# Heads, outputs, norms and projections between two attention layers ordered by a list scheduler, and a last test on one partition

## The chip, the cores and the metric

One core of one Trainium2 chip runs the kernel. The metric is the device time of one execution in microseconds (us), the median over several runs. A profiled execution of the same program gives the trace that the lines below come from; its times count from the start of its span.

## The reference

Four layers on x of 2048 tokens by 512 features, with 32 heads of 16 features each. Layers 1 and 3 are softmax attention with the weights A, layers 2 and 4 linear attention with the weights B and a learned feature map:

```python
x = x + A(layernorm(x)); x = x + B(layernorm(x)); x = x + A(layernorm(x)); x = x + B(layernorm(x))

def A(x):                      # q, k, v = x @ wqkv, by heads
    p = softmax(einsum("bhqd,bhkd->bhqk", q, k) * 16 ** -0.5)
    return einsum("bhqk,bhkd->bhqd", p, v) @ wo

def B(x):                      # q, k, v = x @ wqkv, by heads
    pq, pk = (einsum("bhsd,hdf->bhsf", t, w_phi) for t in (q, k))
    phi_q, phi_k = (concatenate([softmax(p), softmax(-p)]) for p in (pq, pk))
    num = einsum("bhqf,bhfd->bhqd", phi_q, einsum("bhsf,bhsd->bhfd", phi_k, v))
    den = einsum("bhqf,bhf->bhq", phi_q, einsum("bhsf->bhf", phi_k)) + 1e-6
    return (num / den) @ wo
```

## The kernel before

The tokens are cut into 16 tiles of 128, and these into four blocks j of 512 (NJ = 4). Most matrix products are done in three passes of f16 high and low parts (PASSES); TensorE (PE) writes to PSUM, which is divided into two bank pairs of a ring "S" (`psS`), one pair "W" (`double`) and two single banks "M" (`psum1`). `banks` deals out the three pairs in turn.

**The attention layers** (`LayerA`). Eight groups of heads; scores on PE (line 1197), exponentials on ScalarE (ACT, line 1204), products with the values on PE (line 1247). A planner at build time (`Plan`) sets their order and weaves in the projections of later groups ("octets"), the norms of finished groups and the output projection, by costs and due times written in the code. `norms_task` finds a bound on the scores of an octet with a reduction over the partitions on POOL, and writes the bound's negative into `okt` (line 952). At the end of the attention each token block is fed to the next layer.

**The linear layers** (`LayerB`). `feed` takes a token tile at a time: it projects keys, values and queries (line 1549), makes the two softmaxes of the feature map (`expo`, `share`, line 1608 and on), and gathers key times value (`kvp`, in the bank pair W). For the last tile, `blocks` copies kvp into block-diagonal weights `kvb`, and `expo` and `share` are run for its queries; `todo` holds the last two query tiles, which must still be turned over (`turn`). `rest` then runs the heads of block 0, the two turns, and the heads of block 1.

**From one layer to the next** (`finish`). For each token block:
- `heads(j)`: 16 products of turned queries with kvb for each of two halves k, into two bank pairs (line 1693); each pair goes through `norm2` (line 644 and on: ACT copies it, VectorE (DVE) transposes 32 by 32, divides by the denominator and transposes back, ACT makes the high part, POOL (GpSimd) the low part of `obB`).
- `o_block`: the output projection for two halves of two tiles each (lines 675 and 686), with a load of the residual xt (line 662), the sum on DVE (line 691) and a store (line 692). xt has three buffers.
- For a following attention layer: `Norm.half` (layer norm: statistics on DVE, the reciprocal root by three Newton steps of small POOL instructions, lines 492 to 526), the scaled rows on ACT (line 567), their transposes on PE (line 580), high part on ACT and low part on DVE (lines 590 and 593).
- `LayerA.feed`: for each block j the projections of keys and queries of the first octet (`head`, line 828; evacuated by `head_evac`, lines 1099 to 1103), the values (`values0`, line 1005), squares on ACT, their row sums by head (`head_norms`, line 1048) and the bound (`head_bound`). `load_head` and `load_rows` copy the rows of keys and queries from `stg` to the tiles `kq` that the scores read (lines 1176 to 1178), `load_shift` the rows of the bound (line 1184). The first maximum needs the keys of all four blocks and the queries of the first three.

Before, PE's order in this stretch is written out (`manual_schedule(engines={E.PE})`), with the pieces of the next blocks handed to `feed`:

```python
            with tc.manual_schedule(engines={E.PE}):
                outp(0)
                heads(2)
                nxt.feed(lns, [
                    (lambda: outp(1, 0), lambda: outp(1), no),
                    (lambda: heads(3), lambda: outp(2), no),
                    (lambda: outp(3, 0), lambda: outp(3), no),
                    (no, no, no)])
```

The other engines, and all engines behind the last layer, have the order that the builder's own scheduler gives. DMA queues (SP's above all) are ordered by that scheduler in both kernels.

**The last test.** `okt` holds a number per attention layer and octet. If one is below `shmin`, a general version of the whole stack runs in a conditional block; here none is, and the block is jumped over. The lowest value is found on 32 partitions, compared, reduced over the partitions on POOL (`anybad`, line 1850) and converted (line 1852) for the engines to load.

Of the kernel before, what the change touches and what calls it, by code (L numbers as in the profile page):

```python
# [20 lines left out]
H = 32  # L21
# [32 lines left out]
EXP = 0.904  # L54
THERE = 0.54
BACK = 1.11
POWERS = 26
LEAD = 8
RING = 4
# [13 lines left out]
def mha_hedgehog_stack(ctx, tc, x_in, a_wqkv, a_wo, b_wqkv, b_wphi, b_wo, out, shmin=SHMIN):  # L73
# [15 lines left out]
    def big(shape, dt, name):  # L89
        return bigp.tile(shape, dt, tag="big", name=name)  # L90
# [384 lines left out]


    class Norm:
        def __init__(self, xts, name):
            self.xts = xts
            self.xnT = big([P, 2, NC4, 512], F16, f"xnT{name}")  # L480
            self.xn, self.par, self.landed = {}, {}, 0

        def stats(self, t0, n, soon=False):
            run(self.stats_parts(t0, n, soon))
# [127 lines left out]
        def all(self):  # L612
            self.turn01()
            self.turn23()
            return self.xnT
# [115 lines left out]
    class Plan:  # L731
# [59 lines left out]

    class Task:
        pass

    class LayerA:
        def __init__(self, li, x_src, x_dst):
# [311 lines left out]
        def head_values(self, j):  # L1108
            self.values0(j, psum1("pv_"))

        def feed(self, lns, work):

            for j, (a, b, c) in enumerate(work):
                ln = lns[j]
                self.xnT.append(ln.xnT)
                ln.turn01()
                a()
                ln.turn23()
                b()
                c()  # L1120
                if j == 2:
                    self.head_norms(0)
                self.head(j, (1, 0) if j < NJ - 1 else (1,))
                if j == 1:
                    self.next_w = self.octet_w(1)
                    self.load_head()
                if j == 2:
                    self.load_rows(0, slice(1024, AHEAD), None, (nc.sync, nc.gpsimd))
                if j > 0:
                    self.head_values(j - 1)  # L1130
            self.feed_end()

        def load_head(self):

            self.alloc_pairs(0)
            self.shs = [self.shift_tile("yb") for _ in range(2)]
            self.oct[0]["sh"] = self.shift_tile()
            self.kq_end = [np_.tile([P, 2, S - AHEAD], F16, tag="yn", name="kqe", bufs=5) for _ in range(2)]
            self.load_rows(0, slice(0, 1024))
            self.load_shift(0, slice(0, AHEAD), None, (0,))  # L1140

# [236 lines left out]
        def attention(self, extra, nxt):  # L1378
# [127 lines left out]
            print("attention", self.li, "powers", len(power), round(pe, 1), "exponentials", len(estart), "late", round(lost, 1), "ready", self.ready)  # L1506
            self.fill.append(self.last_tail(NJ - 1, self.last))
            state["att"], state["whole"] = False, True
            with tc.manual_schedule(engines=COMPUTE):
# [6 lines left out]
            nxt.rest()  # L1516


    class LayerB:
        def __init__(self, x_src, x_dst, name):  # L1520
            self.x_src, self.x_dst, self.name = x_src, x_dst, name

        def begin(self):
            self.wqk = stgp.tile([P, 2, 2, NC4, 512], F16, tag="stg", name="wbqk")
# [10 lines left out]
        def feed(self, j, xnT, between=lambda t: None):  # L1535

            if self.kvp is None:
                self.kvp = double()
                state["whole"] = False
            qT = [big([P, 4, 512], F32, f"qT{j}_{i}") for i in range(2)]  # L1540
            self.qT.append(qT)
            for t in range(4):
                tt = 4 * j + t

                def project(dst, w, passes=(0, 1, 2)):
                    for i in passes:
# [12 lines left out]
                if last:  # L1559
                    f_k = self.expo(pk)  # L1560
                    self.kvb = np_.tile([P, 8, 32], F32, tag="yn", name="kvb", bufs=5)
                    nc.gpsimd.memset(self.kvb, 0.0)
                else:
                    pq = bank("pq")
                    project(pq, lambda b, c: self.wqk[:, 0, b, c, :])
                if self.lateq is not None and tt < NT - 2:
                    self.turn(*self.lateq)
                pv_ = bank("pbv")
                project(pv_, lambda b, c: self.wv[b][:, c, :])
                if self.latek is not None:  # L1570
                    self.gather(*self.latek)
                if last:
                    pq = bank("pq")
                    project(pq, lambda b, c: self.wqk[:, 0, b, c, :], (0, 1))
                pvh = pv_.rearrange("p (h d) -> p h d", d=DH)
                low = lambda: nc.vector.scalar_tensor_tensor(  # L1576
                    vt[:, 1, :, 0:16], pvh, 2.0 ** -8, vt[:, 0, :, 0:16], op0=ALU.mult, op1=ALU.subtract)
                if not last:
                    f_k = self.expo(pk)
                    f_q = self.expo(pq)  # L1580
                nc.scalar.activation(vt[:, 0, :, 0:16], pvh, AF.Copy, scale=2.0 ** -8)
                if last:
# [4 lines left out]
                    self.blocks()  # L1587
                    self.todo = [self.lateq, (tt, self.expo(pq), qT)]
# [12 lines left out]
                between(tt)  # L1601
# [104 lines left out]
        def finish(self, nxt):  # L1706
# [20 lines left out]
            if not isinstance(nxt, LayerA):  # L1727
# [4 lines left out]
                    if j + 2 < NJ:  # L1732
                        heads(j + 2)
                return
            no = lambda: None
            with tc.manual_schedule(engines={E.PE}):
                outp(0)
                heads(2)
                nxt.feed(lns, [
                    (lambda: outp(1, 0), lambda: outp(1), no),  # L1740
                    (lambda: heads(3), lambda: outp(2), no),
                    (lambda: outp(3, 0), lambda: outp(3), no),
                    (no, no, no)])


    og = tc.dram_tile([D, S], F32, name="og")
# [102 lines left out]
    anybad = sp.tile([32, 1], F32, name="anybad", bufs=1)  # L1849
    nc.gpsimd.partition_all_reduce(anybad, bad, 32, bass_isa.ReduceOp.max)  # L1850
    flag = sp.tile([32, 1], I32, name="flag", bufs=1)
    nc.vector.tensor_copy(flag, anybad)
# [40 lines left out]
```

## Time and profile before

| | us |
|---|---|
| median of 3 runs (lowest, highest) | 2511.46 (2510.26, 2515.81) |
| profiled execution | 2509.21 |
| its span | 2507.3 |
| first attention, scores (line 1204) | from about 70 to 1008 |
| last query projection of the first linear layer to the first score of the second attention | 1187.3 to 1322.9 |
| second attention | 1323 to 2256 |
| last query projection of the second linear layer to the last sum | 2430.4 to 2501.0 |

In lines of the profile, L12 is a line of the kernel, `out<-in` are the program's names for tiles, x is a count, and an arrow with a time says what ended an engine's idle time. PEld is the load of weights into PE, which overlaps its matmuls. In a list of waits the three numbers are the total, the count, and the longest, in us. In the chain of work that ended last each line has start, duration and what ran.

### The profile page before, as it was taken

Reading aid. Unit: us, or ns where it says so; the run is one execution under the profiler, and the core shown is the slowest. Engines: PE = TensorE matmul, PEld = TensorE weight load, DVE = VectorE, ACT = ScalarE, POOL = GpSimd, SP = SyncE. Lnnn points to the kernel's source line nnn. Section 1 sums busy time; section 2 is a strip of 40 time slices with the busy share of each in tenths; the row PEclk is TensorE's granted clock in tenths of the full one; section 3 lists DMA queues with packets and bytes.
Section 4 is the critical chain, followed back from the end, with each engine's and each line's share of the span. In section 5 each row is a group of like instructions: output and inputs, shape, how many; then the busy total and the mean of one; then the engine's idle time right before and its main releaser. Section 6 shows DMA issues by size and latency. Waiting matters only on the chain.

```text
span 2507.3 us, 103429 instructions
## 1 busy us (share of the span) xinstructions
PE 2305.4 (92%) x46698; PEld 1086.9 (43%) x46698; DVE 1596.5 (64%) x2867; ACT 2134.8 (85%) x2379; POOL 531.2 (21%) x645
## 2 busy tenths in 40 slices
PE   6999999999999999889889999999998999998998
PEld 4444444444434444444344444444443344444543
DVE  8233457756668355989863666667565762469897
ACT  6899999999999999454438999999999999993553
POOL 3111111121110000456431112111111100005552
PEclk9999999999999999999899999999999999999999
DMA  5312240231045331100133003203300441210003
GB/s 195 67 27 45 48 80 20 43 55 42 3 114 135 115 109 53 51 9 31 63 96 57 16 7 60 36 3 51 65 3 11 83 125 54 70 68 28 10 18 111
DMA packets 114924, 142.85 MB, mean 57 GB/s; under 512 B 64184, under 2 KB 69928, under 8 KB 112168
## 3 DMA queue, kind: packets, MB, share of 16 engines
q1 hardware_dynamic: 113288, 133.38, 21.6%
q8 instruction: 367, 6.01, 1.0%
q0 software_dynamic: 1184, 2.77, 0.3%
q14 instruction: 85, 0.70, 0.1%
HBM read 62.16 MB, written 41.94 MB: 42 GB/s over the span
## 4 chain that ended last, share of the span: by engine, by line
ACT 58%; PE 14%; issue 13%; DVE 12%; POOL 2%; DMA 0%; POOLq 0%; ACTq 0%; DVEq 0%
ACT p L1204 56%; PE double L1247 2%; PE s L1197 2%; DVE su L1619 2%; PE pbv L1549 1%; PE po L686 1%; PE pk L1549 1%; PE pq L1549 1%; DVE f L1611 1%; PE pm L703 1%; POOL f L1628 1%; DVE f L1612 1%; DVE mx L1608 1%; DVE st L492 1%; DVE su L1620 1%
## 5 line engine op out<-in xcount | busy, mean ns | idle before, releaser
L1204 ACT ACTIVATE p<-s 128x1024 f32<-128x1024 f32 x2001 | 1852.0, 1064 | 21.7 <-PE s L1197 19.1
L1197 PE MATMUL s<-kq 49*32 49x512 f16 x15136 | 789.3, 381 | 99.1 <-ACT p L1204 86.1
L1197 PEld LDWEIGHTS <-kq 49*32 49x32 f16 x15872 | 386.0, 89 | 880.6 <-issue 798.5
L1247 PE MATMUL double<-p,v 64*32 64x512 f32 x9064 | 612.8, 591 | 0.0
L1247 PE MATMUL pm<-p,v 64*32 64x512 f32 x6944 | 476.6, 590 | 0.0
L894 POOL TENSOR_TENSOR yt<-yt,yt 128x512 f32<-128x512 f32 x64 | 84.7, 1324 | 762.8 <-DVE yt L891 727.9
L1247 PEld LDWEIGHTS double<-p,v 64*32 64x32 f32 x9064 | 174.0, 106 | 30.9 <-issue 6.4
L1549 PEld LDWEIGHTS <-xnTa 128*128 128x128 f16 x1152 | 110.6, 98 | 154.9 <-DVE f L1612 26.2
L1281 DVE SCALAR_TENSOR_TENSOR xt<-pm,c_oA,xt 128x512 f32<-128x512 f32 x102 | 76.2, 747 | 155.0 <-PE pm L703 151.1
L1014 POOL TENSOR_TENSOR sq<-stg 128x512 bf16<-128x512 f16 x48 | 57.7, 1202 | 476.4 <-DVE stg L922 247.6
L1628 POOL TENSOR_TENSOR f<-f,su 128x1024 f32<-128x1024 f32 x62 | 119.9, 1934 | 128.3 <-DVE su L1622 102.9
L1247 PEld LDWEIGHTS pm<-p,v 64*32 64x32 f32 x6944 | 135.2, 106 | 22.2 <-issue 3.3
L891 DVE STREAM_TRANSPOSE yt<-double 128x512 f32<-128x512 f32 x72 | 47.3, 695 | 110.7 <-PE double L1247 110.6
L1613 ACT ACTIVATE f<-f,c_pB 128x1024 f32<-128x1024 f32 x64 | 72.7, 1148 | 52.6 <-DVE f L1612 45.4
L1549 PE MATMUL pbv<-wbv,xnTa 128*128 128x512 f16 x384 | 91.6, 390 | 21.4 <-DVE f L1612 21.4
L1634 ACT ACTIVATE fk<-f 128x1024 f16<-128x1024 f32 x30 | 31.7, 1057 | 75.4 <-POOL f L1628 75.4
L703 PEld LDWEIGHTS <-wA 64*32 64x32 f16 x4608 | 76.1, 93 | 43.4 <-issue 7.9
L891 DVE STREAM_TRANSPOSE yt<-pm 128x512 f32<-128x512 f32 x56 | 36.8, 696 | 89.9 <-PE pm L1247 89.6
L1549 PE MATMUL pq<-wbqk,xnTa 128*128 128x512 f16 x384 | 88.4, 379 | 1.6 <-DVE vt L1576 1.6
L917 DVE TENSOR_SCALAR tq<-double,c_qk 128x512 f32<-128x512 f32 x28 | 21.0, 749 | 107.0 <-PE double L703 103.7
L1549 PE MATMUL pk<-wbqk,xnTa 128*128 128x512 f16 x384 | 88.1, 379 | 0.0
L1619 DVE TENSOR_REDUCE su<-f 128x64 f32<-128x1024 f32 x64 | 77.5, 1211 | 9.3 <-ACT f L1613 8.6
(319 smaller groups left out, 3084.7 us busy)
## 6 DMA issues: line engine op xcount, KB each, us to landing
kq<-stg SPq DMA_DIRECT2D x168, 128.0 KB
xd<-xt SPq DMA_DIRECT2D x40, 512.0 KB
xt<-xd SPq DMA_DIRECT2D x40, 512.0 KB
v<-vyt SPq DMA_DIRECT2D x384, 16.0 KB
oD<-osp SPq DMA_DIRECT2D x24, 256.0 KB
ob<-oD SPq DMA_DIRECT2D x8, 768.0 KB
xt<-in_A_x_dram SPq DMA_DIRECT2D x8, 512.0 KB
wbqk<-dBqk SPq DMA_DIRECT2D x2, 2048.0 KB
```

The costliest lines, as they stand in the source:

```text
L703: nc.tensor.matmul(ps[h][c, :], w[r, c], x[r], start=(n == 0), stop=(n == of - 1), skip_group_check=True)
L891: nc.vector.transpose(ys[u].rearrange("p a b -> p (a b)"), ps[u])
L894: nc.gpsimd.tensor_tensor(ys[0], ys[0], ys[1], ALU.add)
L1014: nc.gpsimd.tensor_tensor(sq, hi, hi, ALU.mult)
L1197: nc.tensor.matmul(banks2[u][32 * c:32 * c + 32, :], self.side(g, half, 64 * u, 0, kt * P + 32 * c, 32), self.side(g, half, 64 * u, 1, j * ...
L1204: nc.scalar.activation(pt, s, AF.Exp, scale=EXPS)
L1247: nc.tensor.matmul(acc[h][32 * hh:32 * hh + 32, :], self.oct[o]["v"][r, x:x + 32], pt[r, hh % 2, :], start=(kt == 0), stop=(kt == NT - 1), ...
L1281: nc.vector.scalar_tensor_tensor(xt[:, u, :], ps[h], con["oA"], xt[:, u, :], op0=ALU.mult, op1=ALU.add)
L1549: nc.tensor.matmul(dst, xnT[:, a, c, t * P:(t + 1) * P], w(b, c), start=(i == 0 and c == 0), stop=(i == 2 and c == NC4 - 1))
L1613: nc.scalar.activation(f, f, AF.Exp, scale=con["pB"])
L1619: nc.vector.tensor_reduce(su, f[:, r, :], AX.X, ALU.add)
L1628: nc.gpsimd.tensor_tensor(f3, f3, self.part_sums(f3, slice(0, 64), factor), ALU.mult)
```

## The change

`LayerB.flow` takes the place of `rest` and `finish` on the main path (`b1.flow(a2)`, `b2.flow(None)`); the general version keeps them. It describes the work as tasks, generators that yield the engine and cost of their next instruction ("T" for PE, "V" for DVE, "A" for ACT, "P" for POOL), or a condition: `got` waits for a free buffer or bank, `known` for a result. `Flow.run` keeps a clock for each engine and picks, at each step, the engine whose next instruction can start first, and on it, of the tasks that are due within HOLD, the one of lowest rank. The instruction is emitted at that moment, under a manual schedule of all four engines. Ranks are numbers for each kind of work and block (RANKS between the layers, TAIL behind the last). DMA issues are emitted where their task stands and have no cost there.

- `heads` is cut into calls of eight products (k, p), each into one bank pair.
- `out_block` is cut into the four columns c of heads, and runs each column when that part of obB is ready.
- `norm_in` does the layer norm, the transposes and both parts for two tiles.
- `project`, `square`, `values`, `bounds` and `rows` are the pieces of `LayerA.feed`; `rows` loads the first 1024 columns of kq once the keys and queries of blocks 0 and 1 are out, the next 512 after block 2.
- The queries of the last tile are no longer put through `expo` and `share` in `LayerB.feed`, but in `flow` (`query`), as are the two turns.
- `Norm` can get its tile later (`room`); `load_head` can leave out two kinds of tile (`bound_tiles`, `end_tiles`).
- The last test reads partition 0 of okt alone, without the reduction on POOL.

```diff
+HOLD = 0.1
+RANKS = dict(query=(2,) * 4, heads=(12.4, 3.3, 24, 30.4), out=(10.2, 17.5, 30.6, 25.2), ln=(2.3, -16.8, 14.2, 5.8),
+             keys=(29.8, 57, 32.4, 34.4), project=(59.7, 22.9, -4.7, 53.4), values=(56.3, 0.5, 50, 57.4))
+TAIL = dict(query=(5,) * 4, heads=(4.6, 26.6, 16.2, 25.9), out=(11.1, 5.6, 11.5, 25.9))
...
+        def run(self):
...
+                    due = [t for t in mine if t.ready <= c + HOLD]
+                    t = min(due, key=lambda t: (t.rank, t.ready, t.seq)) if due else min(mine, key=lambda t: (t.ready, t.rank, t.seq))
+                    at = max(c, t.ready)
+                    if best is None or at < best[0]:
+                        best = at, t
+                at, t = best
+                self.end = self.clock[t.need[0]] = at + t.need[1]
...
+            F = Flow(S=[0.5, FAR], W=[1.2], M=[0.0] * 2, p=[0.0] * 5, yn=[0.0] * 4, yb=[0.0] * 2, xt=[0.0] * 3, xn=[0.0] * 4,
+                     sq=[0.0] * 4, big=[0.0, 0.0])
...
+            def heads(j, k, p):
...
+                yield F.got(1, "S", "W")
+                kind, ps = pair()
+                yield "T", 0.9
+                for g in range(4):
+                    for i in (2 * p, 2 * p + 1):
...
+            def out_block(j, t2):
+                yield known(ready, (j, 0))
...
+                yield F.got(1, "xt")
+                F.take("xt")
...
+                nc.sync.dma_start(xt, self.x_src[r:r + 2 * P, :].rearrange("(t p) d -> p t d", p=P))
+                yield F.got(1, "S", "W")
+                kind, ps2 = pair()
+                for c in range(NC4):
+                    yield known(ready, (j, c))
+                    yield "T", 1.3
...
+                yield "V", 1.2
+                nc.vector.scalar_tensor_tensor(xt, ps2, con["oB"], xt, op0=ALU.mult, op1=ALU.add)
...
+            def project(j, ten):
+                yield known(halves, (j, 0), (j, 1))
+                yield F.got(1, "S", "W")
...
+            def bounds():
+                keys = [(j, ten) for j in range(NJ) for ten in (1, 0)]
...
+                for i, need in enumerate((keys[0:4], keys[4:7], keys[7:8])):
+                    yield known(sqs, *need)
...
+            def rows():
+                yield known(evac, *[(j, ten) for j in (0, 1) for ten in (1, 0)])
+                nxt.next_w = nxt.octet_w(1)
+                yield F.got(2, "big")
+                F.take("big"), F.take("big")
+                nxt.load_head(False)
+                yield known(evac, (2, 1), (2, 0))
+                nxt.load_rows(0, slice(1024, AHEAD), None, (nc.sync, nc.gpsimd))
...
-    b1.finish(a2)
+    b1.flow(a2)
     a2.attention(None, b2)
-    b2.finish(None)
...
-    lowest = sp.tile([32, 1], F32, name="lowest", bufs=1)
-    nc.vector.tensor_reduce(lowest, okt, AX.X, ALU.min)
-    bad = sp.tile([32, 1], F32, name="bad", bufs=1)
-    nc.vector.tensor_scalar(bad, lowest, shmin, None, op0=ALU.is_lt)
-    anybad = sp.tile([32, 1], F32, name="anybad", bufs=1)
-    nc.gpsimd.partition_all_reduce(anybad, bad, 32, bass_isa.ReduceOp.max)
-    flag = sp.tile([32, 1], I32, name="flag", bufs=1)
-    nc.vector.tensor_copy(flag, anybad)
+    lowest = sp.tile([1, 1], F32, name="lowest", bufs=1)
+    nc.vector.tensor_reduce(lowest, okt[0:1], AX.X, ALU.min)
+    flag = sp.tile([1, 1], I32, name="flag", bufs=1)
+    nc.vector.tensor_scalar(flag, lowest, shmin, None, op0=ALU.is_lt)
     rv = nc.values_load(flag[0:1, 0:1], min_val=0, max_val=1)
```

More of the change, by code (lines that the diff above doesn't have):

```diff
@@ L793, in mha_hedgehog_stack, with __init__, add, pull @@
         pass
+    class Flow:
+        def __init__(self, **free):
+            self.clock = {"T": 0.0, "V": 0.5, "A": 0.5, "P": 0.0}
+            self.free, self.tasks, self.count, self.end = free, [], 0, 0.0
+        def add(self, gen, rank, ready=0.0):
+            t = Task()
+            t.gen, t.rank, t.ready, t.need, t.cond, t.last, t.seq = gen, rank, ready, None, None, None, self.count
+            self.count += 1
+            self.tasks.append(t)
+            self.pull(t)
+        def pull(self, t):
+            while True:
+                try:
+                    need = next(t.gen)
+                except StopIteration:
+                    self.tasks.remove(t)
+                    return
+                if need[0] == "until":
+                    at = need[1]()
+                    if at is None:
+                        t.cond, t.need = need[1], None
+                        return
+                    t.ready = max(t.ready, at)
+                    continue
+                if t.last is not None and t.last != need[0]:
+                    t.ready += 0.25 if t.last == "T" else 0.08
+                t.need = need
+                return
+        def got(self, n, *names):
+            def at():
+                times = sorted(x for name in names for x in self.free[name])
+                return times[n - 1] if len(times) >= n else None
+            return "until", at
+        def take(self, *names):
+            name = min((name for name in names if self.free[name]), key=lambda name: min(self.free[name]))
+            self.free[name].remove(min(self.free[name]))
+            return name
+        def give(self, name, n=1, wait=0.1):
+            self.free[name] += [self.end + wait] * n
+        def run(self):
+            while self.tasks:
+                for t in sorted(self.tasks, key=lambda t: (t.rank, t.seq)):
+                    if t.cond is not None:
+                        at = t.cond()
+                        if at is not None:
+                            t.cond, t.ready = None, max(t.ready, at)
+                            self.pull(t)
+                best = None
+                for e, c in self.clock.items():
+                    mine = [t for t in self.tasks if t.need is not None and t.need[0] == e]
+                    if not mine:
+                        continue
+                    due = [t for t in mine if t.ready <= c + HOLD]
[5 more added lines that the diff above has]
+                self.end = self.clock[t.need[0]] = at + t.need[1]
+                t.ready, t.last = self.end, t.need[0]
+                t.need = None
+                self.pull(t)
@@ L1109, in head_values, with bound_tiles, end_tiles, load_head @@
             self.values0(j, psum1("pv_"))
[L1111 to L1133, printed above, removed]
+        def bound_tiles(self):
+            self.shs = [self.shift_tile("yb") for _ in range(2)]
+        def end_tiles(self):
+            self.kq_end = [np_.tile([P, 2, S - AHEAD], F16, tag="yn", name="kqe", bufs=5) for _ in range(2)]
+        def load_head(self, every=True):
             self.alloc_pairs(0)
-            self.shs = [self.shift_tile("yb") for _ in range(2)]
+            if every:
+                self.bound_tiles()
             self.oct[0]["sh"] = self.shift_tile()
-            self.kq_end = [np_.tile([P, 2, S - AHEAD], F16, tag="yn", name="kqe", bufs=5) for _ in range(2)]
+            if every:
+                self.end_tiles()
             self.load_rows(0, slice(0, 1024))
@@ L1505, in attention @@
             assert not plan.tasks and not events
-            print("attention", self.li, "powers", len(power), round(pe, 1), "exponentials", len(estart), "late", round(lost, 1), "ready", self.ready)
             self.fill.append(self.last_tail(NJ - 1, self.last))
             state["att"], state["whole"] = False, True
+            nxt.fixed = True
             with tc.manual_schedule(engines=COMPUTE):
@@ L1515, in attention @@
                     nxt.feed(j, self.out[j], lambda t: self.pumps(3 if t < 4 else t > 4))
-            nxt.rest()
     class LayerB:
@@ L1521, in __init__ @@
             self.x_src, self.x_dst, self.name = x_src, x_dst, name
+            self.fixed = False
         def begin(self):
```

302 lines of the change are left out of this document (290 added, 12 removed).

## The prediction

> **What bounds the kernel now.** I read the page first (busy shares, chain), then the busy time of the three stretches that the diff touches, then who waits for whom in each.
>
> ```profile
> span 2507.3 us, 103429 instructions
> PE 2305.4 (92%) x46698; PEld 1086.9 (43%) x46698; DVE 1596.5 (64%) x2867; ACT 2134.8 (85%) x2379; POOL 531.2 (21%) x645
> ACT  6899999999999999454438999999999999993553
> ACT 58%; PE 14%; issue 13%; DVE 12%; POOL 2%; DMA 0%; POOLq 0%; ACTq 0%; DVEq 0%
> L1204 ACT ACTIVATE p<-s 128x1024 f32<-128x1024 f32 x2001 | 1852.0, 1064 | 21.7 <-PE s L1197 19.1
> ```
>
> ACT carries the two softmax attentions (the runs of 9 in its row; line 1204 alone is 1852 us). The diff leaves their work as it is, apart from what the last test did in the middle of the second. The rest of the diff lies in the two stretches where ACT's digits fall to 3 to 5: behind the first linear-attention layer (I call it the bridge: from its last query projection to the first scores of the second attention) and behind the second (the tail).
>
> ```profile
> core 0: us, PE busy (x) PEld busy (x) DVE busy (x) ACT busy (x) POOL busy (x), PEclk, DMA share, GB/s
> 1187.30:1322.90 135.60, 112.47 (x825) 54.97 (x825) 102.88 (x193) 55.42 (x77) 53.46 (x145) 0.89 0.27 84
> 2430.40:2501.00 70.60, 61.00 (x464) 23.95 (x464) 60.54 (x97) 29.27 (x41) 23.12 (x18) 0.95 0.31 106
> 2501.00:2507.30 6.30, 0.00 (x0) 0.00 (x0) 0.00 (x0) 0.00 (x0) 0.00 (x0) 0.67 0.26 91
> ```
>
> Columns: length, then busy us of PE, PEld, DVE, ACT, POOL, then the granted clock. In the bridge DVE works 102.88 of 135.60 us (76%) and PE 112.47 at a granted clock of 0.89, which is about 100 us at full clock. In the tail both are at 86%. No engine is full, so both stretches lose time to order. The last 6.30 us are the final store, which the change doesn't touch.
>
> **The bridge.** Its instructions stay nearly the same in kind and number: heads, norms, output projections, layer norms, transposes, projections. What changes is who orders them. Now PE's order is written by hand and the other engines' order is chosen by the builder; afterwards one list scheduler fixes PE, DVE, ACT and POOL together, by a rank for each kind of work and token block. DVE's 102.88 us therefore stay. What can go is DVE's idle time, 32.7 us:
>
> ```profile
> DVE xnTb L593 <- ACT xnTb L590: 9.7, 2, 5.9
> DVE tq L1099 <- PE pqk L828: 7.0, 3, 3.3
> DVE xt L691 <- PE double L686: 6.0, 1, 6.0
> DVE yt L646 <- ACT raw L644: 3.9, 2, 2.9
> DVE xt L691 <- PE po L686: 3.8, 1, 3.8
> ```
>
> The first, third and fifth are waits in the middle of the bridge (together 19.5 us), where other blocks have DVE work that could stand there: the 32 transposes, multiplies and evacuations of four blocks don't depend on each other. The second stands at the end:
>
> ```profile
> 1307.84 1.22 DVE L593 TENSOR_TENSOR xnTb<-double,xnTb 128x1024 f16<-128x1024 f32 x1
> 1307.63 4.44 PE pqk L828 x12
> 1312.07 2.68 PE pv__26758 L1005 x48
> 1314.75 2.60 PE pqk L828 x12
> 1318.13 0.68 DVE nm L1049
> 1320.83 2.06 DMA kq<-sh
> 1322.93 0.55 PE s L1197 x8
> ```
>
> From the end of the last evacuation of normed rows (1309.06) to the first score (1322.93) are 13.9 us. PE puts the values of block 2 (2.68) and the last query projection (2.60) ahead of the row sums whose maximum (line 1049) gives the softmax bound; the new order gives the last key projection a better rank (34.4) than values (50) and that query projection (53.4), so these 5.3 us leave the chain. The key projection takes 4.44 where the same twelve matmuls take 2.60 at full clock: 1.8 more can go. Against it, square and row sums of that last key block now follow one another, some 2 us: the row sums and their maximum take 1.5 now, from the end of the query projection (1317.35) to 1318.81, and half a microsecond is my estimate for the square. So the end would be 13.9 - 5.3 - 1.8 + 2 = 8.8 us.
>
> Floor of the bridge: 102.9 of DVE and nearly all of that end, 8.5 us, 111.4 in all, a gain of 24. The other bound is no gain, or a loss, if the fixed order stalls somewhere. The nearest row for what a simple order reaches is the tail, 60.54 of 70.60: at that share 102.88 need 119.7, a gain of 15.9; half the way to the floor is 12.1. I take 13 (122.6 us), nearer the lower, because PE is as full as DVE: 100 us at full clock plus the same end.
>
> PE's own cost changes at one place. The heads come in calls of eight matmuls on two row groups instead of sixteen on four:
>
> ```profile
> 1187.30:1322.90 135.60, 20.73 (x256) 3.34 (x256) 0.89 0.27 84
> 2433.26 1.09 PE L1693 MATMUL pn<-qT,kvb 32*32 32x512 f32 x16 [0.46 <-DVE f L1612]
> 2460.41 1.14 PE L1693 MATMUL pn<-qT,kvb 32*32 32x512 f32 x32
> ```
>
> A call of eight (16 records) takes 1.09, a call of sixteen 1.14, so all sixteen calls of a layer take 17.4 us split and 9.1 whole. The bridge now has 20.73 us of them, since the halves go apart there already when only one bank pair is free. I cost the split at nothing; if PE were the only bound and the whole calls could be had, it would be 8.3.
>
> The clock is a second place. In two stretches of the bridge:
>
> ```profile
> 1220.00:1230.00 10.00, 5.42 (x39) 1.95 (x40) 5.87 (x12) 5.69 (x7) 4.97 (x27) 0.50 0.33 106
> 1260.00:1270.00 10.00, 10.00 (x49) 5.12 (x49) 10.00 (x18) 4.47 (x6) 3.00 (x3) 0.96 0.00 0
> ```
>
> Where PE is half idle the granted clock is 0.50, where it is full 0.96. I let the 0.89 of the whole stand in the sum: with it PE has 112 us and is the tighter of the two bounds. [...]
>
> **Queues.** SP's order isn't fixed by the scheduler, but its work is moved:
>
> ```profile
> 1279.78 1.30 SPq L1176 DMA_DIRECT2D kq<-stg  x1
> 1287.57 0.59 SPq L1178 DMA_DIRECT2D kq<-stg  x1
> 1224.74 0.37 SPq L662 DMA_DIRECT2D xt<-xd  x1
> ```
>
> The first rows of keys and queries are twelve copies on SP, from 1279.78 to 1288.16, 8.4 us. They need the queries of block 0, whose rank (59.7) is the worst of all. Now they lie 35 us ahead of the first score and cost nothing. If that evacuation came last, the first score would follow it by 8.4 and the 2.06 of a landing, 10.5 us, against 8.8 for the chain of the bound: 2 us more, within what I left of the floor. On POOL the six later copies stand in the fixed order behind the evacuations of block 2; what waits behind them is the layer norm's small arithmetic of block 3, but POOL has 53.46 busy of 135.60 us, so I cost them at nothing, and at their own issue time, some 3 us, if a norm stands right behind them. The eight loads of xt (0.37 to issue) have no time in the scheduler's model. Six matmuls for each of four columns stand before their first use; they are the rival that makes the kernel slower.
>
> **The tail.** The same work without layer norms.
>
> ```profile
> DVE xt L691 <- PE po L686: 7.9, 2, 4.0
> 2491.26 8.39 PE po L686 x38
> 2499.67 1.28 DVE xt L691
> ```
>
> DVE has 60.54 of 70.60 us; 7.9 of its idle time are the last two output blocks, for which PE still has 38 matmuls (8.39 us) when the last head is ready. The new order runs the columns of both output blocks as they come, so that only the last column of each is left, two times 1.3 (a block half has 24 matmuls, 8.39 / 38 x 24 = 5.3 us, and a column is a quarter of it). Floor: 60.5, 1.7 at the start, and 4.4 at the end: 66.6, a gain of 4. PE has 61.00 at a clock of 0.95, 58 us, and can't start its outputs before the first heads are normed, so the floor is hardly reached. No gain is the other bound, 2 lost if a column waits in the fixed order. I take 2.
>
> **The last test.** Now a partition reduction on POOL and a conversion behind it; afterwards a minimum on one partition and a comparison that writes the integer. The builder puts the old one not at the end but into the second attention, at 1927 to 1942:
>
> ```profile
> POOL yt L894 <- issue: 7.2, 1, 7.2
> DVE flag L1852 <- POOL anybad L1850: 7.2, 1, 7.2
> POOL anybad L1850 <- issue: 6.0, 1, 6.0
> ACT p L1204 <- PE s L1197: 6.0, 2, 4.9
> PE double L1197 <- DVE yt L891: 4.9, 1, 4.9
> ```
>
> Read from below: PE waits 4.9 us for a transpose on DVE, which stands behind the flag, which waits 7.2 us for the reduction, ahead of which POOL has 6.0 us without a record; ACT, the bound there, stands 6.0 us. POOL needs another 7.2 us before its next add. In the whole of each attention ACT waits for scores this long:
>
> ```profile
> ACT p L1204 <- PE s L1197: 6.5, 14, 1.2
> ACT p L1204 <- PE s L1197: 12.5, 9, 4.9
> ```
>
> The first is the attention without that test, the second the one with it; they differ by the same 6.0. Without reduction the flag follows the minimum at once, the transpose runs when its bank is full, and the 6.0 go; the minimum still waits for the last bound on POOL, which costs DVE 4 us that nothing needs. The bounds are 0 (the builder puts the new instructions where they stall something else) and 7.3 (a later wait of 1.3 goes as well). I take 6.0. The two new instructions cost two short ones on DVE in place of three.
>
> **The sum.** 13 + 2 + 6 = 21 us off the profiled execution, 2509.2 us with 1.9 around its span: 2488.2. The median of the three runs shown is 2511.5, 2.3 above it, so I predict 2490.5, rounded 2490. A measurement of this kernel can tell about 0.2%, 5 us, from no change.
>
> **Rivals.**
> - The bridge comes to its floor because PE keeps its full clock: 24 + 4 + 6 = 34, 2477. For it: the rows of the clock, and independent work in plenty. Against: three bank pairs have to carry heads, outputs, transposes and projections, and no stretch of this kind here exceeds 86%. Chance 0.10.
> - The fixed order stalls head-on as often as the present one: one late instruction holds its whole engine. The bridge gives 3, the tail nothing, the test 6: 2502. For it: PE's order has been fixed already and lost 23 us in the bridge. Chance 0.20.
> - Slower: loads of xt. With three buffers the loads of five of eight output halves can only start when an earlier half is through its norm. A half megabyte at the 84 to 106 GB/s of these stretches is 5 to 6.2 us, and DVE, in its fixed order, stands still for what isn't covered. It eats the gain of 21 from 4.2 us uncovered for each of the five, and is slower by 0.2% from 5.2; uncovered in full at 5.4 it gives 27, 2517. Against: each load is issued before 5.3 us of matmuls of its own block. Chance 0.05.
> - The change doesn't do what it says: the new minimum still holds DVE where PE needs it, and the bridge stays where it is: 2511 within 0.2%. For it: the wait of the minimum for POOL stays. Chance 0.09.
>
> **How the numbers follow.** My forecast has 0.56. Faster by over 0.2% are it and the first two rivals, 0.86, of which I give 0.01 to the slower side for a stall that I haven't named: 0.85, 0.09, 0.06. The forecast's own range, by a bridge gain of 7 to 19 and a tail of 0 to 4, is 2482 to 2498. The range from 2477 to 2504 takes in both faster rivals and leaves out the last two.
>
> **What would show it.** Bridge: under 125 us from the last query projection to the first score, DVE's share over 80%, PE's clock over 0.93, and no values between the last key projection and its row sums. Tail: the wait of xt for po under 4 us. Test: no anybad, and ACT's wait for scores in the second attention 6 to 7 us. Wrong would be a DVE wait for a load of xt, a first score that waits for rows of stg instead of the bound, or a bank wait that holds PE while DVE is idle.

## The result and the profile after

The changed kernel took 2495.93 us (median of 6 runs, 2493.94 to 2498.00), the kernel before 2512.52 (6 runs beside them): 16.6 us less, ratio 0.9934 [0.9921, 0.9947]. On a second chip it was 2495.67 against 2516.21, ratio 0.9925 [0.9906, 0.9944] (e12_after_2 below; a ratio is worked out from all runs of both kernels and can differ from the quotient of the medians). The forecast was 21 off the profiled execution, 2490, in a range of 2477 to 2504.

Stages of profiled executions, cut as in the prediction, but with the bridge up to the first exponential (0.5 us behind the first score). "Feed" is a linear layer up to its last query projection. Attention and feeds of other executions of the same code are beside them to show how well such a row repeats:

| us | before | after | again on another chip |
|---|---|---|---|
| to the end of the first attention | 1008.77 | 1009.35 | 1010.08 |
| feed of the first linear layer | 178.56 | 178.33 | 178.48 |
| bridge | 136.17 | 124.02 | 124.94 |
| second attention | 933.22 | 928.12 | 929.53 |
| feed of the second linear layer | 173.68 | 175.33 | 175.08 |
| tail | 70.55 | 70.64 | 69.47 |
| final store | 6.35 | 6.41 | 6.42 |
| span | 2507.3 | 2492.2 | 2494.0 |

The bridge gave 12.15 and the second attention 5.1; the tail gave nothing here, and 1.65 went in a feed whose code the change hardly touches. Two of these rows move by themselves: over all profiled executions here the second feed took 173.6 to 175.7, and the second attention 933.2 to 937.7 with the old test (five executions) and 926.2 to 931.0 with the new one (nine).

The page of the changed kernel, and the busy time by stage (length, then PE, PEld, DVE, ACT, POOL, then the granted clock):

```profile
span 2492.2 us, 103433 instructions
PE 2303.5 (92%) x46698; PEld 1083.9 (43%) x46698; DVE 1602.2 (64%) x2866; ACT 2136.6 (86%) x2379; POOL 530.6 (21%) x644
ACT  6899999999999999444539999999999999993553
```

```profile
1187.70:1311.20 123.50, 106.24 (x825) 51.81 (x825) 107.18 (x191) 55.65 (x77) 54.12 (x145) 0.94 0.22 67
2415.50:2485.80 70.30, 63.29 (x464) 23.83 (x448) 62.41 (x96) 29.54 (x41) 22.57 (x18) 0.95 0.26 91
2485.80:2492.20 6.40, 0.00 (x0) 0.00 (x0) 0.00 (x0) 0.00 (x0) 0.00 (x0) 0.77 0.25 90
```

In ACT's row the last slice between the attentions goes from 8 to 9 tenths; a slice is 62 us, so 12 us shows as no more. Engines do the same work. In the bridge DVE's share went from 76% to 87%, PE's clock from 0.89 to 0.94, and its busy time fell by 6.2 us with the same 825 matmuls. DVE's own busy time rose by 4.3 us, so its idle time fell from 32.7 to 16.3. What DVE still waits for in the bridge:

```profile
DVE xnTb L603 <- ACT xnTb L600: 5.1, 2, 3.2
DVE xt L1953 <- PE fl L1950: 3.4, 2, 3.1
DVE nm L1132 <- PE psn L1131: 2.2, 1, 2.2
DVE tq L2047 <- PE double L911: 1.0, 1, 1.0
```

The waits of 9.7, 7.0, 6.0, 3.9 and 3.8 us of before are 5.1 and 3.4 (xnTb, xt), 1.6 (tq, 0.6 of it in a further line for `fl`), and none (yt). No wait for a load of xt is among them. The end of the bridge, from the chain of work that ended last:

```profile
1296.66 1.03 ACT xnTb L600
...
1297.74 2.75 PE double L911 x12
1300.49 2.59 PE fl L911 x12
1303.08 2.68 PE pv__26779 L1088 x48
1305.76 0.77 PE psn L1131 x3
...
1306.55 0.68 DVE nm L1132
...
1308.97 2.12 DMA kq<-sh
...
1311.13 0.55 PE s L1266 x8
```

PE goes through the key projection (`double`, 2.75), the query projection (`fl`, 2.59), the values (2.68; they are those of block 3 now) and only then the row sums. The last evacuation of normed rows ends at 1298.95, the first score starts at 1311.13: 12.2 us, against 13.9 before.

The tail, the end of its chain and DVE's waits:

```profile
2476.79 0.49 POOLq L2241
2477.28 0.71 POOL obB L1930
...
2478.04 1.25 PE fl L1950 x5
2479.29 5.19 PE double L1950 x24
...
2484.51 1.28 DVE xt L1953
```

```profile
DVE xt L1953 <- PE double L1950: 3.9, 1, 3.9
DVE xt L1953 <- PE fl L1950: 2.9, 3, 1.3
```

The last output half has all its 24 matmuls (5.19) behind the other one's last column; DVE waits 3.9 us for them. In all it waits 6.8 for outputs here, 8.1 before; the prediction wanted under 4.

The last test, and ACT's wait for scores from the end of the bridge on, with the longest one (4.8) that for the first score itself:

```profile
1917.85 0.15 DVE L2238 TENSOR_REDUCE lowest<-okt 1x1 f32<-1x8 f32 x1 [4.09 <-POOL okt L1035]
1918.04 0.14 DVE L2240 TENSOR_SCALAR flag<-lowest 1x1 int32<-1x1 f32 x1
```

```profile
ACT p L1273 <- PE s L1266: 7.4, 7, 4.8
```

The minimum still holds DVE for 4.09 us, and nothing but DVE pays for it: beside it ACT runs 18 exponentials without a gap (1909.15 to 1925.91). The first score has no such wait of 4.8 in the kernel before (2.0); without it ACT waits 2.6 here and waited 10.5 before.

### The profile page after: what moved, and what is told of

The parts are those of the page before. It is cut to its first block, busy times and chain, and to the rows that moved or that the text cites. A ratio compares the mean times of both kernels' runs of the same rounds, so it can differ in the third digit from the quotient of the medians.

```text
span 2492.2 us, 103433 instructions
## 1 busy us (share of the span) xinstructions
PE 2303.5 (92%) x46698; PEld 1083.9 (43%) x46698; DVE 1602.2 (64%) x2866; ACT 2136.6 (86%) x2379; POOL 530.6 (21%) x644
## 4 chain that ended last, share of the span: by engine, by line
ACT 58%; PE 14%; issue 12%; DVE 12%; POOL 2%; DMA 0%; ACTq 0%; POOLq 0%; SPq 0%; DVEq 0%
ACT p L1273 57%; PE double L1316 3%; PE s L1266 2%; DVE su L1691 1%; PE pbv L1618 1%; PE pk L1618 1%; PE pq L1618 1%; PE pm L713 1%; DVE yt L1908 1%; DVE f L1683 1%; POOL f L1700 1%; DVE f L1684 1%; PE fl L1950 1%; DVE mx L1680 1%; PE pm L1316 1%
## 5 line engine op out<-in xcount | busy, mean ns | idle before, releaser
L1700 POOL TENSOR_TENSOR f<-f,su 128x1024 f32<-128x1024 f32 x58 | 112.2, 1934 | 116.3 <-DVE su L1694 103.4
L1950 PE MATMUL fl<-wbo,obB 128*128 128x512 f16 x312 | 76.7, 403 | 8.7 <-ACT raw L1902 3.6
```

What stands on the lines that cost most here:

```text
L1700: nc.gpsimd.tensor_tensor(f3, f3, self.part_sums(f3, slice(0, 64), factor), ALU.mult)
L1950: nc.tensor.matmul(ps2[:, u, :], obs[j][:, c, a, t * P:(t + 1) * P], wo[:, b, c, :], start=(c == 0 and i == 0), stop=(c == NC4 - 1 and i = ...
```

## The experiments

The ratios are to the kernel before, run on the same chip. Theory throughout: three independent gains, bridge about 12, test about 5, tail none.

### e1_test: the last test alone

```diff
-    lowest = sp.tile([32, 1], F32, name="lowest", bufs=1)
...
-    nc.gpsimd.partition_all_reduce(anybad, bad, 32, bass_isa.ReduceOp.max)
...
+    lowest = sp.tile([1, 1], F32, name="lowest", bufs=1)
+    nc.vector.tensor_reduce(lowest, okt[0:1], AX.X, ALU.min)
```

> The kernel before with the last test on one partition and nothing else. Theory: the POOL reduction in the second attention held DVE and through it PE; without it ACT's idle time there falls, and the second attention gets shorter by the 5.2 us that it lost in the changed kernel (933.3 to 928.1 from first to last exponential): 5 us off the time. Rival: the gain came from somewhere else in the new bridge (another start of the second attention), and the test alone gives under 2 us.

2507.51 (9 runs) against 2513.66 (25 runs), ratio 0.9975 [0.9965, 0.9985]: 6.2 us. The second attention took 926.48 (933.22 before). ACT's wait for scores in it:

```profile
ACT p L1204 <- PE s L1197: 6.2, 6, 2.6
```

12.5 became 6.2. The prediction's 6.0 stands.

### e2_bridge: the scheduled bridge alone

```diff
-    b2.flow(None)
+    b2.finish(None)
```

and the old test.

> The list scheduler between the first linear layer and the second attention alone; old tail, old test. Theory: the bridge is 123.5 us instead of 135.6, all else as before: 12 us off. Rival: a part of the 12 us is given back when the second attention starts (rows of keys that come late), so that the time falls by 8 or less.

2513.79 (11 runs), ratio 1.0003 [0.9994, 1.0012]: nothing, though the bridge was 124.96. The tail, whose code is that of before, took 80.19 in place of 70.55, and the second attention 937.65, the longest of the five with the old test. What PE and ACT wait for in this tail:

```profile
PE double L1767 <- ACT raw L654: 11.5, 3, 5.6
```

```profile
ACT raw L654 <- PE pn L1767: 11.0, 2, 9.7
```

And in the chain:

```profile
2466.98 10.47 PE po L696 x48
2478.74 1.03 ACT raw L654
```

Of block 3 the halves of heads had only begun when 48 output matmuls of earlier blocks got ahead of them: ACT, which copies the heads, stood 9.7 us. Both theories missed this, and the parts aren't independent. `banks` deals out the three bank pairs by a counter; the old bridge draws 40 pairs from it, the scheduled one none (it names its pairs itself). In the attention and in the linear layer's feed the counter is switched off (`whole`), so the old tail goes on from where the bridge left it. 40 is 1 more than a multiple of 3, so that tail gets its pairs in another turn. The next two runs test that.

### e5_bridge_turn and e6_before_turn: the counter alone

```diff
+    state["turn"] = (state["turn"] + 1) % 3
```

behind the scheduled bridge (e5), and by 2 ahead of the second attention in the kernel before (e6).

> The scheduled bridge alone, as in the run before it, with one step added to the counter that deals out the three bank pairs in turn. The old bridge drew 40 pairs from that counter, the scheduled one draws none, so that the old tail began one step off (40 is 1 more than 3 times 13) and took 80.2 us instead of 70.6. Theory: with the step put back the tail is 70.6 us again and the time falls by 9 to 10 us against the bridge alone, to about 2504. Rival: the tail was longer for another reason (its order by the builder hangs on times further back), it stays near 80 us and the time near 2513.

> The kernel before, with the counter of bank pairs set two steps on ahead of the second attention and nothing else changed. Theory: its tail starts at the place in the turn that the run with the scheduled bridge alone had, takes 80 us instead of 70.6, and the kernel gets 9 to 10 us slower (2523). Rival: no change.

e5: 2502.72 (8 runs) against 2515.29 (13 runs), ratio 0.9957 [0.9942, 0.9972], tail 70.64. e6: 2524.78 (5 runs), ratio 1.0041 [1.0029, 1.0054], tail 80.15, with the same wait to the tenth:

```profile
ACT raw L644 <- PE pn L1693: 11.0, 2, 9.7
```

So one turn of a round robin is worth 9.6 us in the old tail, and the bridge by itself, with the counter put right, is worth 12.6 by the medians and 10.8 by the ratio. The scheduled tail chooses its own pairs: in the full change it doesn't gain over the old one, but it keeps away the 9.6 that the scheduled bridge would have brought upon it.

### e3_tail: the scheduled tail alone

> The list scheduler behind the last linear layer alone; old bridge, old test. Theory from the trace of the changed kernel: the tail stays at 70.6 us, no change within 1 us. Rival, the step of the prediction: 2 us off.

2511.67 (11 runs), ratio 0.9995 [0.9985, 1.0004]; tail 69.62. No gain that can be told from none by the times. The stage shows a little: five executions with the scheduled tail as in the changed kernel took 69.5 to 70.6 (69.8 on average), three with the old one in its usual turn 70.6 to 70.8.

### e4_xt: the last output half

```diff
-                    F.give("xt", 1, 4.0)
+                    F.give("xt", 1, 0.1)
```

(in the tail: when the scheduler counts an xt tile as free, after its sum; the store behind it was counted at 4.0.)

> The changed kernel with one number changed: in the tail a buffer of xt counts as free 0.1 us after its sum instead of 4.0. Theory: the last output half had to wait in the scheduler's model for a buffer of xt, so that its 24 matmuls (5.2 us) stand alone at the end; with the number its columns run as the heads come, and the tail is 3 us shorter than in the changed kernel, 2493 in all (DVE then waits some for the load). Rival 1: the wait was for a bank pair, and nothing changes. Rival 2: DVE waits for the loads in its fixed order, and the tail gets longer by 1 to 3 us.

2495.05 (5 runs), ratio 0.9925 [0.9911, 0.9938], tail 69.13; again, as e11_xt_2 below, 68.34. The end of the chain in that one:

```profile
2474.81 0.22 PE double L1950
2475.03 1.29 PE fl L1950 x6
2476.32 2.59 PE double L1950 x12
2478.91 1.31 PE fl L1950 x6
...
2480.25 1.28 DVE xt L1953
```

Both halves now go column by column, as the prediction had it. It gives 1.1 to 1.5 us of the 3 expected: in that execution PE is busy without a gap from 2463.28 to its end, so the columns of one half only change places with those of the other.

### e8_block_ranks: the same scheduler with plain ranks

```diff
-RANKS = dict(query=(2,) * 4, heads=(12.4, 3.3, 24, 30.4), ...
+RANKS = dict(query=(2,) * 4, heads=(10, 20, 30, 40), ...   # and so for every kind
```

> The changed kernel, with ranks between the layers that follow the block alone (10, 20, 30, 40 for all kinds of work of blocks 0 to 3, 2 for the queries as before). Theory: most of the gain comes from filling DVE's waits with work of another block, which any order of ranks does; the bridge is 126 to 131 us and the time 2499 to 2503. Rival: it is the searched ranks that gain, and the bridge falls back to the 136 us of the kernel before.

2504.54 (6 runs), ratio 0.9968 [0.9955, 0.9980]; the bridge took 136.02, as long as the handwritten one. Its busy times, and what stopped DVE most:

```profile
1190.70:1326.20 135.50, 109.60 (x832) 53.35 (x831) 106.42 (x191) 55.60 (x77) 52.23 (x145) 0.89 0.26 77
```

```profile
DVE xnTb L602 <- ACT xnTb L599: 11.8, 3, 7.7
DVE tq L2046 <- PE fl L910: 5.4, 2, 3.2
DVE xt L1952 <- PE double L1949: 4.7, 3, 2.4
```

The largest waits are of the same kinds as before (xnTb, tq, xt), and DVE's idle time is 29.1 us, against 32.7 before and 16.3 in the changed kernel. The rival is right for this one set of plain ranks: the gain of the bridge comes with the order that the changed kernel's ranks give, not with the scheduling of four engines together. The 8 us that remain by the ratio are, within its interval, the last test.

### e7_gate_xt, and e9 to e12: the values behind the row sums

The end of the bridge was expected to lose the values (2.68) and the query projection (2.60). Here the values of block 3 may not start until the row sums for the first bound are placed, with e4's edit as well:

```diff
             def values(j):
                 yield known(halves, (j, 0), (j, 1))
+                if j == NJ - 1:
+                    yield known(halves, "bound")
...
                         nxt.head_norms(i)
...
                     if i == 1:
+                        halves["bound"] = F.end
```

> The changed kernel with the buffer number of the tail (0.1 instead of 4.0), and the values of block 3 held back until the row sums for the first bound are issued. Theory: the 2.7 us of values that PE put between the last query projection and those row sums go into its wait for the rows of the bound (3.8 us), the bridge is 2.5 us shorter, 121.5 to the first exponential, and the time is 2.5 us below that of the buffer number alone (2495), 2492.5. Rival: the row sums then wait for the square of the last keys or for another transfer, and under 1 us is won.

2489.48 (4 runs), ratio 0.9899 [0.9885, 0.9914], the lowest of any run here. But its profiled execution had a bridge of 124.69, not 121.5. Hence the edit, its partner, the pair and the changed kernel once more, on one (other) chip, with 2516.21 before:

> The changed kernel with one line more in its scheduler: the values of block 3 may not start before the row sums for the first bound have been placed. Its pair (values held and the last output half's tile counted free at once) was timed 5.6 us under the kernel with the free tile alone, but in its profiled execution the bridge was 124.69 us, 0.9 longer than the other's 123.76. Theory: holding the values is worth nothing, since the bridge didn't shorten; the difference was one of chips and runs. Then this one is the changed kernel within 2 us, 0.993 to 0.994 of the kernel before, bridge 124 to 125.5, and no values between the last key projection and its row sums. Rival: the values do cost their 2.68 us, or more, and the profiled execution of the pair was a late one: then this one lies 3 to 6 us under the changed kernel, 0.991 to 0.992, bridge 121 to 122.

> The pair again, on the same chip as its two halves and the changed kernel. Theory (the held values are worth nothing): the same as the free tile alone within 2 us, 0.992 to 0.993 of the kernel before. Rival (they are worth about 5): 0.990, 5 us under the free tile alone.

> The changed kernel with the last output half's tile counted free at once, again. Its tail was 69.13 against 70.64 in the profile. Theory (the tail is worth its 1.5 us and no more): 1 to 2 us under the changed kernel on this chip. Rival (what the pair showed comes from here): 4 to 6 us under it.

> The changed kernel as it is, the base of the other three on the same chip. Both theories: 0.9921 to 0.9947 of the kernel before. Its bridge (to the first exponential) was 124.02 and its tail 70.64; if the profile's stages repeat within 1 us, the three others are to be read against these.

| | us (6 runs each) | ratio | last evacuation to first score | bridge |
|---|---|---|---|---|
| e12, the changed kernel | 2495.67 | 0.9925 [0.9906, 0.9944] | 12.9 | 124.94 |
| e11, free tile | 2494.24 | 0.9919 [0.9904, 0.9933] | 12.8 | 125.18 |
| e9, values held | 2494.22 | 0.9919 [0.9903, 0.9934] | 9.9 | 123.37 |
| e10, both | 2489.50 | 0.9903 [0.9886, 0.9919] | 10.4 | 122.56 |

PE at the end of the bridge in the pair (e10):

```profile
1297.75 2.76 PE L911 MATMUL double<-xnTb,wA 128*128 128x512 f16 x12
1300.35 2.75 PE L911 MATMUL fl<-xnTb,wA 128*128 128x512 f16 x12
1303.04 0.82 PE L1131 MATMUL psn<-sq,bones 128*32 128x512 bf16 x3
1303.79 2.85 PE L1088 MATMUL pv__26827<-wAv,xnTb 128*128 128x128 f16 x48
1306.58 0.39 PE L1131 MATMUL psn<-sq,bones 128*32 128x512 bf16 x1
1308.84 0.97 PE L1266 MATMUL s<-kq 49*32 49x512 f16 x16 [1.87 <-DMA kq<-sh]
```

The values have left the chain and stand where PE would wait for the bound. Over all executions of this bridge the end took 9.9, 10.4 and 11.0 with the edit, 12.2 twice, 12.8 and 12.9 three times without (e2 and e5 among them): 2.2 us. Of that the whole bridge shows 1.1 (123.5 against 124.6 on average): the stretch ahead of the end, whose code is the same, took 111.0 to 111.7 without the edit and 111.6, 112.9 and 113.1 with it. In the longest of these (e7) the granted clock was 0.90 instead of 0.94; in the other it was 0.94, and why it was longer is open. Neither part alone can be told from the changed kernel; both together were 6.2 us under it beside it, and 5.6 under e4 in the earlier runs (e7, on a chip other than e4's), which is more than the two parts and more than the stages show. The intervals of pair and parts overlap, so whether that is a sum of 2 and chance or something more is open. The theory that holding the values is worth nothing doesn't stand either: the end of the bridge is shorter each time.

## Why the prediction was right, and where its steps were not

- **The bridge**, forecast 13: 12.15 in the profile, 12.6 alone (e5; 10.8 by the ratio). Waits in the middle went as said, DVE's share is above 80%, the clock above 0.93, the length 123.45 to the first score against a limit of 125. But two terms were off, in opposite directions, and so was the reason, so that the 13 was in part luck. The end is 12.2, not 8.8: the step that failed is that values and query projection leave the chain. The ranks do put the last key projection first, and the row sums (rank 53.4) ahead of the values of block 3 (57.4); but a rank decides only among tasks that are due, the square of those keys needs an evacuation and ACT first, and in that time the scheduler's model finds PE free and gives it both. With the values held (e10) the square of the last keys (0.63; the prediction's estimate was 0.5) ends at 1302.49 and the row sums begin at 1303.04, behind the query projection, and their maximum waits until 1304.36 behind DVE's evacuation of it: the query projection costs some 1.0 us there, by this estimate, not 2.60, since most of it lies beside that evacuation and square. The values were the larger part, 2.2 us (e7, e9, e10). And DVE's 102.88 didn't stay: 107.18. The idle time shrank by 16.4 instead. Two small readings were off as well: of the 19.5 us of waits "in the middle" 3.8 stood at 1306.7, at the end, and at the tail's share 102.88 need 120.0, not 119.7; the 13 hangs on neither.
- **The reason for it.** The prediction took a common list scheduler to fill DVE's gaps by itself, from the tail's share of 86%. With plain ranks it doesn't (e8): 136.02. The forecast rested on a ratio that these ranks happened to reach, which is luck.
- **The clock.** It was left standing at 0.89; it came to 0.94, and PE's busy time from 112.47 to 106.24. The bridge's gain doesn't hang on it: in e7 the same scheduled bridge, its values held, ran at 0.90 and took 124.69. What sets the clock isn't shown. In the changed kernel it was 0.50 from 1199 to 1212, behind gaps of PE of 1.39 and 1.17 us, and stayed there while PE was full:

```profile
1198.36 1.40 PE L1866 MATMUL pqt<-ident,f 128*128 128x128 f32 x8 [1.39 <-POOL f L1859]
1200.92 3.36 PE L1889 MATMUL fl<-qT,kvb 32*32 32x512 f32 x32 [1.17 <-ACT raw L1902]
```

```profile
1199.00:1202.00 3.00, 1.83 (x21) 0.58 (x18) 2.97 (x7) 2.75 (x4) 0.00 (x0) 0.50 0.00 0
1207.00:1212.00 5.00, 5.00 (x13) 1.76 (x12) 4.89 (x6) 3.09 (x4) 2.48 (x2) 0.50 0.00 0
```

So the prediction's reading of two rows, 0.50 where PE is half idle and 0.96 where it is full, doesn't hold in general: here PE is full at 0.50. The rival that had PE at its full clock, the floor of 2477, didn't come: the clock was 0.94, with no gap of PE over 2.3 us until its last wait (3.8), DVE's own work grew by 4.3, and DVE kept 16.3 us of waits.
- **Heads, queues, loads**: nothing of these is seen to hold the bridge. There is no DVE wait for a load of xt and no first score that waits for rows of stg; the rival on the slower side never showed.
- **The tail**, forecast 2: nothing that the times show (e3), 70.64 against 70.55 in the profile, 0.8 by the averages of the stage. The step that failed is that "only the last column of each is left". A single number of the scheduler, 4.0 us until a tile of xt is free, kept the last half back whole; with it gone the step holds, and is worth 1.1 to 1.5 (e4, e11), since PE is full there to the end. What the prediction didn't see at all is that bridge and tail hang together by the counter of bank pairs: with the old tail behind the new bridge 9.6 of its gain are lost there, and in the times all of it (e2).
- **The last test**, forecast 6.0: 6.2 alone (e1). In the full change the second attention gained 5.1, but that is one pair of executions: on average five with the old test took 934.9 and nine with the new one 928.2, 6.7 less. ACT's idle time in it fell by 6.5; the same 997 exponentials, and nothing else on ACT, took 923.19 against 921.84, and between 921.8 and 923.2 in the other executions, for which no run shows the reason.
- **The sum**: 12.15 + 5.1 - 0.1 - 1.65 in the feed, less 0.4 elsewhere, is the 15.1 between the spans; the medians differ by 16.6, on the other chip by 20.5 (18.9 by the ratio). The 5.9 between the 21 forecast and those 15.1 are the tail's 2.1, the feed's 1.65, the attention's 0.9, the bridge's 0.85 and 0.4 ahead of the feeds and behind the tail; the feed's and the attention's parts are no more than these stages vary by between executions.

## What to carry to other kernels

When a stage is ordered anew, what it draws from any rotating resource sets the phase for whatever draws from it next: put the counter back, or time the stage with everything behind it fixed, before judging the edit. A list scheduler's gain is in its priorities and in the few costs of its model; one set of plain ranks gave the handwritten time, and one wrong release time cost the tail its gain. Look where a chain waits for a small result (a bound, a flag): what stands on the engine between must be work that is needed no earlier, and it must be told to the scheduler, since its ranks won't say it.

## What the runs showed that was not expected

The feed of the second linear layer took 173.6 to 175.7 us in the variants of the changed kernel, whose code there is the same. Two of them (the changed kernel, then e10) differ in the granted clock:

```profile
2239.82:2415.15 175.33, 160.38 (x1140) 84.46 (x1131) 157.84 (x252) 79.08 (x101) 102.82 (x107) 0.98 0.06 19
```

```profile
2238.94:2412.79 173.85, 159.16 (x1140) 83.89 (x1131) 157.46 (x252) 78.86 (x100) 102.71 (x107) 0.99 0.06 20
```

Of all fourteen profiled executions here the five in which this feed ran at 0.98 or less took 175.1 or more. But of the nine at 0.99 seven took 173.6 to 173.9 and two 174.9 and 175.0 (e6, e3), so the clock isn't all of it. No edit of 1.5 us can be read from one profile.

Of DVE's added 4.3 us in the bridge 1.6 are the multiply that divides the heads (yn, 16 times): a median of 648 ns in both kernels, but 831 on average after and 728 before. In the changed kernel (start, duration, engine):

```profile
1207.20 0.65 DVE L1918 TENSOR_TENSOR yn<-yt,rec 128x512 f32<-128x512 f32 x1
...
1208.59 2.69 DVE L1918 TENSOR_TENSOR yn<-yt,rec 128x512 f32<-128x512 f32 x2
...
1209.41 1.33 POOL L1930 TENSOR_TENSOR obB<-yb,obB 128x512 f16<-128x512 f32 x1 [0.23 <-ACT obB L1928]
```

Two that fall beside POOL's subtractions take 2.69 instead of 1.30. Of the 32 multiplies in both kernels the six that took over 1.1 us all ran beside such a subtraction for 0.59 us or more; those with nothing on POOL beside them, or only its small instructions, took 0.63 to 0.69. One (before, at 1203.71) ran beside a subtraction throughout and took 0.64, so the overlap alone doesn't decide. What else does, no run here shows.

The flag of the last test is loaded by each engine's queue, by all but SP's near the end of the kernel (2476.1 to 2484.5); on POOL that took 0.49 us right ahead of the last `obB`, in the chain of the tail. No run took it away.
